# Batch 0 of a hash-masked attention: the fifth chunk's weight sums to TensorE, key-bit copies and mask products from VectorE to ScalarE

## The chip, the cores and the metric

The kernel runs on one core of a Trainium2 chip. The metric is device microseconds (us) of one execution. Engines are named as in the profile: PE (TensorE), PEld (its weight loads), DVE (VectorE), ACT (ScalarE), POOL (GpSimd) and SP (SyncE, which here only issues DMAs). Each engine works through its own instructions in program order, and engines meet through semaphores.

## The reference

Four batches, eight heads, 768 positions, head width 64. Six random projections give each query and key a six-bit bucket; a query sees only the keys of its own bucket.

```python
q_bits = (np.einsum('bhsd,dk->bhsk', q, proj) > 0)      # k_bits alike
mask = q_bucket[:, :, :, None] == k_bucket[:, :, None, :]
scores = scale * np.matmul(q, k.transpose(0, 1, 3, 2))
scores = np.where(mask, scores, -1000000000.0)
attn = softmax(scores); out = attn @ v
...
u = x + real(fft2(x))                 # x: (4, 768, 512), the heads side by side
un = (u - mean(u)) / sqrt(var(u) + 1e-6)
return u + relu(un @ w_ch1) @ w_ch2   # 512 -> 2048 -> 512
```

The first half is the attention, the second a Fourier mixing with a two-layer network behind it.

## The kernel before

**The whole.** The four batches follow each other. Attention works on pairs of heads: pair number n = 4 b + t, for t = 0 to 3. While the attention of batch b runs, the Fourier mixing and the network of batch b-1 are threaded between its steps. Batch 0 has no such partner, so its attention is threaded with the arrival of w_ch1 (`weights1`, line 728). Batch 0 is the stage that the change touches. It stands inside `manual_schedule` (line 1534): for PE, DVE, ACT and POOL the order is the one in which the Python code issues the instructions, and a scheduler has no say. From batch 1 on a scheduler orders them.

**One step of attention.** A pair has six steps, c = 0 to 5, one for each chunk of 128 keys. In a step:

- PE computes the scores of the chunk against all 768 queries, in two halves g of 384 queries. For each half and each of the two heads there is first a bf16 matmul of the bit rows (line 938), which adds a large constant where buckets agree, and then the fp32 score matmul (line 946). Both go to one PSUM tile `sc`, of which there are two, so half g of a step cannot start until ACT has read the same half of the step before.
- ACT takes the exponential of each half (line 950) into `pk`, of which there are two buffers. Where buckets differ the result is zero.
- DVE adds the new weights into `acc` (line 1041), in two halves. From c = 1 to 4 it does so in batch 0; the last chunk, c = 5, is not added but summed by PE.
- PE multiplies the weights with the values (line 967), one step late: in step c it does the products of chunk c-1, after the scores of chunk c.

So PE's order is: scores c, products c-1, then whatever else the step brings, then scores c+1. After the sixth chunk (in the first step of the next pair) ACT copies the products out (lines 977 and 980), PE sums `acc` and the last `pk` over the keys with a matrix of ones (line 985), and DVE turns the sums (line 992) and takes their reciprocals; a step later ACT copies these into place (line 1001), and DVE scales the output (lines 1002 and 1006).

**Preparing the next pair** (`prepare`, line 807) is threaded into steps 1 to 4 of the pair before, one part a step: DVE transposes q (c = 1) and k (c = 2) (line 820); then for q (c = 3) and for k (c = 4) PE computes the projections (line 854) and DVE turns them into bits (line 858). Pairs 0 to 4 are prepared in a light way (`LITE`): the bits of q are multiplied with the two columns of `own`, which leave a large number or zero (line 864, two instructions), and the bits of k are copied with 32-row blocks exchanged (line 870, four instructions). The scores of the next pair need the q products and the k bits for half g = 0, and the copies for half g = 1.

**Arrival of w_ch1.** The weights come as raw 64-bit words. Each of 16 slices is turned into fp32 by two bit operations on DVE (lines 639 and 643), a conversion of the low word on ACT (line 647), and an addition on DVE (line 649) that needs ACT's part. A slice is converted in four of five steps. After four slices PE sums columns of w_ch1 (`ws`, line 673), ACT copies the sums (`part`, line 678), PE averages (`wm`, line 681), and DVE subtracts the mean (line 687). In batch 0 this happens in pair 0 and pair 1 as they end; for the other two column blocks PE's part follows when the attention of batch 0 is over.

**Small PSUM tiles.** The bit projections, `ws`, `wm` and the sums take turns in two PSUM buffers (`pt`, line 520), so each waits until the tile two places earlier has been read.

**Pair 3** has one thing more on DVE: the first half of the Fourier folding, 3.2 us ahead of the q bits of pair 4 and 3.2 us ahead of its k bits (`fold`, lines 1099 to 1117).

The order of one step is set here:

```python
pk = weigh(n, c)                 # scores, exponentials
...                              # additions into acc
for sc in scales: next(sc, None)
while pending: finish()          # products of the chunk before
pending.append((n, c, pk, oos, sums))
if c > (3 if b == 1 else 2): next(half, None)     # fold, pair 3
if c > 0: next(ahead, None)                       # prepare(n + 1)
yield                                             # -> one slice of w_ch1
```

Of the kernel before, what the change touches and what calls it, by code (L numbers as in the profile page):

```python
# [16 lines left out]
AF = mybir.ActivationFunctionType  # L17
ALU = mybir.AluOpType
AX = mybir.AxisListType

P = 128
B, H, S, D = 4, 8, 768, 64
# [3 lines left out]
NT = S // P  # L26
NPAIR = H // 2
HALF = S // 2
# [457 lines left out]
def _main(  # L486
# [33 lines left out]
    def pt(shape, name):  # L520

        turn[0] += 1
        if roomy[0] and turn[0] % 2:
            if turn[0] % 4 == 1:
                return ps_o.tile(shape, F32, tag="o", name=name)
            return ps_sc.tile(shape, F32, tag="sc", name=name)
        return ps_1.tile(shape, F32, tag="ps", name=name)
# [279 lines left out]
    def prepare(n):  # L807

        lite = n in LITE
        ts = {}  # L810
        for io, nm in enumerate("qk"):
            tn = nat.pop((nm, n))
            tt = wt([P, S], F32, nm + "t", f"{nm}t{n}")
            if n > 0:
                to, at = tt, tn
                if nm == "q":

                    to = tt.rearrange("p (i r n) -> p r i n", i=2, r=2)
                    at = tn.rearrange("p (r i n) -> p r i n", i=2, r=2)
                nc.vector.transpose(to, at)  # L820
            for g in range(2) if n == 0 else ():
                ps = pt([P, 3, P], f"tr{nm}{n}_{g}")
                for i in range(3):
                    c = 2 * i + g if nm == "q" else 3 * g + i
                    nc.tensor.transpose(ps[:, i, :], tn[:, c * P : (c + 1) * P], ident)
                if nm == "q":
                    for i in range(2):
                        dst = tt[:, i * HALF + g * HALF // 2 : i * HALF + (g + 1) * HALF // 2]
                        evac(
                            dst.rearrange("p (j c) -> p c j", c=3),  # L830
                            ps[:, :, i * D : (i + 1) * D],
                        )
                else:
                    evac(
                        tt[:, g * HALF : (g + 1) * HALF],
                        ps.rearrange("p c t -> p (c t)"),
                    )
            ts[nm] = tt
            yield
            if n >= LATER:  # L840
                norm(n, io, tn)
        if lite:

            qk = wt([P, 2, S], BF16, "qb", f"qkb{n}")
            qz = qk[:, 0].rearrange("p (g s) -> p g s", g=2)
            bits = {"q": qz[:, 0], "k": qk[:, 1, 0:HALF]}
            for io, nm in enumerate("qk"):  # L850
                ps = pt([P, HALF], f"bits{nm}{n}")
                for j in range(4):
                    h, g = divmod(j, 2)
                    nc.tensor.matmul(
                        ps[32 * j : 32 * j + 32, :], pjw[:, h * D : h * D + 32],
                        ts[nm][:, g * HALF : (g + 1) * HALF], start=True, stop=True,
                    )
                nc.vector.tensor_scalar(
                    bits[nm], ps, 0.0, off[:, io : io + 1],
                    op0=ALU.is_gt, op1=ALU.subtract,  # L860
                )
                if io == 0:
                    for g in (1, 0):
                        nc.vector.tensor_scalar(
                            qz[:, g], qz[:, 0], own[:, g : g + 1], None, op0=ALU.mult
                        )
                else:
                    for j in range(4):
                        to, at = (slice(32 * i, 32 * i + 32) for i in (j, j ^ 1))
                        nc.vector.tensor_copy(qk[to, 1, HALF:S], qk[at, 1, 0:HALF])  # L870
                yield
            preps[n] = ts["q"], ts["k"], qk, None
            return

        ps = pt([P, HALF], f"bits{n}")
        for j in range(4):
            src = ts["qk"[j // 2]][:, (j % 2) * HALF : (j % 2 + 1) * HALF]
            nc.tensor.matmul(
                ps[32 * j : 32 * j + 32, :], pj, src, start=True, stop=True
            )  # L880
        bt = wt([P, HALF], BF16, "bt", f"bt{n}")
        nc.vector.tensor_scalar(bt, ps, 0.0, None, op0=ALU.is_gt)  # L882
        yield

        qb = wt([P, 2, S], BF16, "qb", f"qb{n}")
        kb = wt([P, 2, NT], F32, "kb", f"kb{n}")
        for h in range(2):
            ps = ps_sc.tile([P, 2, 512], F32, tag="sc", name=f"qb{n}_{h}")
            for g in range(2):
                rows = slice(32 * g, 32 * g + 32)  # L890
                with behind() if g + h else nullcontext():
                    last[0] = nc.tensor.matmul(
                        ps[:, g, 0:HALF], pw[rows, h, :], bt[rows, :],
                        start=True, stop=True,
                    )
            evac(qb[:, h, :].rearrange("p (g s) -> p g s", g=2), ps[:, :, 0:HALF])
        ps = ps_sc.tile([P, 2, 512], F32, tag="sc", name=f"kb{n}")
        for c in range(NT):
            g, i = divmod(c, NT // 2)
            rows = slice(64 + 32 * g, 96 + 32 * g)  # L900
            with behind() if c else nullcontext():
                last[0] = nc.tensor.matmul(
                    ps[:, g, 2 * i : 2 * i + 2], bt[rows, i * P : (i + 1) * P],
                    pw[rows, :, 0], start=True, stop=True,
                )
        nc.vector.tensor_copy(
            kb.rearrange("p h (g i) -> p g i h", g=2),
            ps[:, :, 0:NT].rearrange("p g (i h) -> p g i h", h=2),
        )
        preps[n] = ts["q"], ts["k"], qb, kb  # L910
# [58 lines left out]
                    pk[:, g, h, 0:w], start=(c == 0), stop=(c == NT - 1),  # L969
                )  # L970

    def scale(n, oos, sums):


        x = xs[n // NPAIR][:, n % NPAIR]
        vs = wt([P, 1], F32, "vs", f"vs{n}")
        nc.scalar.copy(vs, oos[0][:, HALF : HALF + 1])
        halves = [x[:, g * HALF : (g + 1) * HALF] for g in range(2)]
        for g, xg in enumerate(halves):
            nc.scalar.activation(xg, oos[g][:, 0:HALF], AF.Identity, bias=vs)  # L980

        ps = pt([P, HALF], f"sum{n}")
        for i, part in enumerate(sums):
            for j in range(4):
                nc.tensor.matmul(
                    ps[32 * j : 32 * j + 32, :], ones, part[:, j // 2, j % 2],
                    start=(i == 0), stop=(i == len(sums) - 1),
                )


        rt = wt([P, S], F32, "rt", f"rt{n}", 1)
        nc.vector.transpose(rt[:, 0:HALF], ps)  # L992
        rc = wt([P, HALF // 32], F32, "rc", f"rc{n}")
        nc.vector.tensor_scalar(rc, rt[:, 0:HALF:32], S * EPS, None, op0=ALU.add)
        nc.vector.reciprocal(rc, rc)
        yield
        rr = wt([P, 2, HALF // 32], F32, "rr", f"rr{n}")
        for g in range(2):
            for i in range(4):
                j = 2 * g + i // 2  # L1000
                nc.scalar.copy(rr[32 * i : 32 * i + 32, g], rc[32 * j : 32 * j + 32])
        nc.vector.transpose(
            rt.rearrange("p (j i) -> p j i", i=32),
            rr.rearrange("p g j -> p (g j)")[:, :, None].broadcast_to([P, S // 32, 32]),
        )
        nc.vector.tensor_tensor(x, x, rt, op=ALU.mult)

    def attention(b):
        xs[b] = wt([P, NPAIR, S], F32, "x", f"x{b}")
        pending, scales = [], []  # L1010

        def finish():
            n, c, pk, oos, sums = pending.pop(0)
            with behind() if n >= NPAIR and t is not None else nullcontext():
                values(n, c, pk, oos)
            if c == NT - 1:
                scales.append(scale(n, oos, sums))
                next(scales[-1])

        for t in range(NPAIR):  # L1020
# [8 lines left out]
            for c in range(NT):  # L1029
# [2 lines left out]
                sums = [acc]  # L1032
                if c == 0:
                    first = new
                elif c == NT - 1 and b == 0:

                    sums.append(new)
                else:

                    for g in (0, 1) if b == 0 else (slice(0, 2),):  # L1040
                        nc.vector.tensor_tensor(  # L1041
                            acc[:, g], (first if c == 1 else acc)[:, g], new[:, g],
                            op=ALU.add,
                        )
# [590 lines left out]
```

## Time and profile before

| what | value |
|---|---|
| three runs | 1115.38, 1116.21, 1119.01 us; median 1116.21 |
| the profiled execution: its time | 1115.38 us |
| the profiled execution: span from the first to the last instruction | 1113.5 us |
| granted clock of PE over the span | 0.989 |
| instructions in the span | 14,170 |
| first scores of pair 0 | 11.71 us after the start |
| first scores of pair 4 (batch 1) | 119.27 us after the start |

The median of the runs lies 0.8 us above the profiled execution. Its time is 1.9 us more than its span; that part is outside the instructions.

A line of the timeline gives the start, the time that it covers, the engine, the line of the kernel, the operation, what is written and read, the shapes, how many instructions are merged, and in brackets how long the engine sat idle before it and whom it waited for. A line of the waits gives the waiting engine and line, the one waited for, then the total in us, the number of waits and the longest. In a table of stretches, each engine has its busy time and, in brackets, its instructions; behind them stands the granted clock. Matmuls overlap, so PE's busy time does not say how much of its time is used; the distance from the start of a group to the start of the next one does. A group of four score matmuls of one half of a step takes 0.81 us this way, with the bit matmuls inside it.

### The profile page before, as it was taken

How to read it: one execution, taken by the hardware profiler on the slowest of the kernel's cores; microseconds unless marked ns; L12 is line 12 of the kernel's file. 1: busy time of each engine (PE TensorE's matmuls, PEld its weight loads, DVE VectorE, ACT ScalarE, POOL GpSimd, SP SyncE). 2: the span in 40 equal slices, each digit the busy share in tenths (PEclk: the TensorE clock that was granted, in tenths of full speed). 3: DMA queues.
4: the chain of work that ended last, by engine and by line, in shares of the span. 5: the costliest groups of instructions: out<-in, count | busy, mean ns of one | idle time of the engine just before them, and what ended most of it. 6: DMA issues, size and time to landing. Idle time of an engine off the chain costs nothing. (4 is left out here: it accounts for less than half of the span.)

```text
span 1113.5 us, 14170 instructions
## 1 busy us (share of the span) xinstructions
PE 1050.3 (94%) x4933; PEld 632.6 (57%) x4933; DVE 789.8 (71%) x1336; ACT 499.8 (45%) x1055; POOL 76.2 (7%) x164
## 2 busy tenths in 40 slices
PE   7899897899999999999999999999899999899996
PEld 3333354447644675555754685545564579568675
DVE  6889969768798968767767867776476785444353
ACT  4555455562376233545145324454635423851420
POOL 0000000001000120010000020010200012400000
PEclk9989999999999999999999999999999999999999
DMA  9754362540156260323153160323542206732401
GB/s 237 221 90 103 57 173 68 193 105 1 38 138 217 57 194 11 67 76 67 56 142 88 39 186 31 62 62 95 174 162 64 65 24 229 260 112 78 131 20 41
DMA packets 179295, 117.82 MB, mean 106 GB/s; under 512 B 130064, under 2 KB 163472, under 8 KB 179216
## 3 DMA queue, kind: packets, MB, share of 16 engines
q1 hardware_dynamic: 169840, 88.65, 29.7%
q0 software_dynamic: 7808, 27.79, 7.7%
q8 instruction: 41, 0.67, 0.3%
q10 hardware_dynamic: 1568, 0.39, 0.2%
q14 instruction: 38, 0.31, 0.1%
HBM read 95.82 MB, written 20.97 MB: 105 GB/s over the span
## 5 line engine op out<-in xcount | busy, mean ns | idle before, releaser
L1323 PE MATMUL o<-w,h 128*128 128x256 f32 x1152 | 262.1, 384 | 5.3 <-DVE rt L992 1.9
L1323 PEld LDWEIGHTS o<-w,h 128*128 128x128 f32 x1152 | 217.1, 191 | 50.4 <-issue 4.0
L950 ACT ACTIVATE pk<-sc 128x768 f32<-128x768 f32 x192 | 149.6, 810 | 100.1 <-PE sc L946 79.2
L1443 PE MATMUL h_p<-x,w 128*128 128x384 f32 x448 | 165.3, 498 | 4.8 <-ACT h L1465 3.7
L946 PE MATMUL sc<-qt,kt 64*128 64x384 f32 x768 | 155.9, 508 | 4.5 <-ACT pk L950 4.2
L967 PE MATMUL oo<-pk,vn 128*64 128x385 f32 (+1 forms) x768 | 155.6, 502 | 4.3 <-DVE pk L956 3.6
L956 DVE SCALAR_TENSOR_TENSOR pk<-qb,kb,pk 128x768 f32<-128x768 bf16 x132 | 129.0, 1012 | 39.2 <-ACT pk L950 35.6
L1443 PEld LDWEIGHTS h_p<-x,w 128*128 128x128 f32 x448 | 82.4, 192 | 73.2 <-ACT h L1465 7.5
L1443 PE MATMUL h_p<-w 128*128 128x384 f32 x288 | 106.3, 491 | 6.5 <-ACT w L1480 3.4
L1041 DVE TENSOR_TENSOR acc<-acc,pk 128x1536 f32<-128x1536 f32 (+1 forms) x72 | 105.7, 1482 | 5.7 <-ACT pk L950 5.2
L967 PEld LDWEIGHTS oo<-pk,vn 128*64 128x64 f32 x768 | 49.7, 137 | 99.1 <-issue 73.7
L946 PEld LDWEIGHTS sc<-qt,kt 64*128 64x128 f32 x768 | 67.0, 188 | 50.8 <-issue 24.5
L1443 PEld LDWEIGHTS h_p<-w 128*128 128x128 f32 x288 | 53.8, 191 | 46.7 <-ACT w L1480 5.4
L1335 DVE SCALAR_TENSOR_TENSOR w<-o,rs,w 128x256 f32<-128x256 f32 x56 | 26.7, 478 | 39.0 <-PE o L1323 38.9
L1353 ACT COPY tq<-o 128x256 f32<-128x256 f32 x24 | 8.9, 371 | 94.2 <-PE o L1323 94.2
L1469 DVE TENSOR_TENSOR h<-h 128x384 f32<-128x384 f32 x32 | 17.8, 557 | 40.9 <-ACT h L1468 40.9
L1323 PE MATMUL o<-w 128*128 128x256 f32 x176 | 42.3, 383 | 1.3 <-DVE w L1335 1.3
L1476 DVE TENSOR_TENSOR h<-h 128x384 f32<-128x384 f32 x32 | 17.7, 553 | 32.5 <-ACT h L1475 32.4
L1077 POOL DMA_DIRECT2D out_dram<-w x30 | 16.4, 548 | 334.9 <-DVE w L1335 184.4
L1323 PEld LDWEIGHTS o<-w 128*128 128x128 f32 x176 | 32.8, 190 | 8.8 <-DVE w L1335 2.9
L1342 ACT COPY tq<-o 128x256 f32<-128x256 f32 x24 | 8.9, 370 | 60.6 <-PE o L1323 60.5
L1139 PE MATMUL cs<-ch,z 128*128 128x128 f32 (+3 forms) x192 | 32.3, 318 | 2.3 <-DVE bt L882 1.9
(175 smaller groups left out, 1330.6 us busy)
## 6 DMA issues: line engine op xcount, KB each, us to landing
w<-ad SPq DMA_DIRECT2D x168, 128.0 KB, 2.0
w<-bd SPq DMA_DIRECT2D x42, 512.0 KB, 4.5
zraw<-in_moe_w_ch_dram POOLq DMA_DIRECT2D x16, 512.0 KB, 4.1
zlast<-in_moe_w_ch_dram POOLq DMA_DIRECT2D x16, 512.0 KB, 5.1
bd<-w SPq DMA_DIRECT2D x14, 512.0 KB, 3.6
vn<-in_v_dram SPq DMA_DIRECT2D x32, 192.0 KB, 3.5
qn<-in_q_dram SPq DMA_DIRECT2D x120, 48.0 KB, 2.4
kn<-in_k_dram SPq DMA_DIRECT2D x60, 96.0 KB, 3.3
```

What stands on the lines that cost most here:

```text
L946: last[0] = nc.tensor.matmul(ps[:, h, 0:HALF], kt[rows, ks], qt[rows, qs], start=kb is not None, stop=True,)
L950: nc.scalar.activation(pk[:, g, :, 0:HALF], ps[:, :, 0:HALF], AF.Exp, scale=SCALE)
L956: nc.vector.scalar_tensor_tensor(w, qb[:, h].rearrange("p (g s) -> p g s", g=2), kb[:, h, c : c + 1], w, op0=ALU.is_equal, op1=ALU.mult,)
L967: nc.tensor.matmul(oos[g][h * D : (h + 1) * D, 0:w], nat["v", n][:, (2 * c + h) * D : (2 * c + h + 1) * D], pk[:, g, h, 0:w], start=(c == ...
L1041: nc.vector.tensor_tensor(acc[:, g], (first if c == 1 else acc)[:, g], new[:, g], op=ALU.add,)
L1077: (nc.sync if b == B - 1 else nc.gpsimd).dma_start(out[b, s0 : s0 + 2 * w - 1 : 2, cols], src[at : at + w, cols])
L1139: nc.tensor.matmul(ps[:, pc + 2 * lo : pc + 2 * hi - 1 : 2], z[:, cp, pc, par, t * P : (t + 1) * P], ch[:, cp, pc, lo:hi], start=(cp == 0) ...
L1323: nc.tensor.matmul(ps, a[:, r], right7[i][:, r], start=start and r == 0, stop=r == HF // 2 - 1, skip_group_check=not start,)
L1335: nc.vector.scalar_tensor_tensor(t[:, cols], src, r, t[:, cols], op0=ALU.mult, op1=ALU.add)
L1443: nc.tensor.matmul(ps, left[:, k], right[i][:, k], start=start and k == 0, stop=k == 1, skip_group_check=not start,)
L1469: nc.vector.tensor_tensor(c21, c12, c21, op=ALU.add)
L1476: nc.vector.tensor_tensor(c22, c21, c22, op=ALU.add)
```

## The change

In batch 0 three kinds of work change engine. The two products of the q bits with the columns of `own` and the four copies of the k bits become ACT instructions, in all five lightly prepared pairs. The additions of the fifth chunk (c = 4) into `acc` are left out for the four pairs of batch 0; PE sums that chunk with the matrix of ones instead, into the PSUM tile that later takes the sums of `acc` and of the sixth chunk. That tile is taken one step earlier than before.

```diff
                 if io == 0:
                     for g in (1, 0):
-                        nc.vector.tensor_scalar(
-                            qz[:, g], qz[:, 0], own[:, g : g + 1], None, op0=ALU.mult
+                        nc.scalar.activation(
+                            qz[:, g], qz[:, 0], AF.Copy, scale=own[:, g : g + 1]
                         )
                 else:
                     for j in range(4):
                         to, at = (slice(32 * i, 32 * i + 32) for i in (j, j ^ 1))
-                        nc.vector.tensor_copy(qk[to, 1, HALF:S], qk[at, 1, 0:HALF])
+                        nc.scalar.copy(qk[to, 1, HALF:S], qk[at, 1, 0:HALF])
...
+    def weight_sums(ps, sums, first, last):
+
+        for i, part in enumerate(sums):
+            for j in range(4):
+                nc.tensor.matmul(
+                    ps[32 * j : 32 * j + 32, :], ones, part[:, j // 2, j % 2],
+                    start=first and i == 0, stop=last and i == len(sums) - 1,
+                )
+
-    def scale(n, oos, sums):
+    def scale(n, oos, sums, ps=None):
...
-        ps = pt([P, HALF], f"sum{n}")
-        for i, part in enumerate(sums):
-            for j in range(4):
-                nc.tensor.matmul(
-                    ps[32 * j : 32 * j + 32, :], ones, part[:, j // 2, j % 2],
-                    start=(i == 0), stop=(i == len(sums) - 1),
-                )
+        fresh = ps is None
+        if fresh:
+            ps = pt([P, HALF], f"sum{n}")
+        weight_sums(ps, sums, fresh, True)
...
+            if b == 0 and c == NT - 2:
+                total.append(pt([P, HALF], f"sum{n}"))
+                weight_sums(total[0], sums[:1], True, False)
             if c == NT - 1:
-                scales.append(scale(n, oos, sums))
+                scales.append(scale(n, oos, sums, total.pop() if total else None))
...
                 if c == 0:
                     first = new
+                elif c == NT - 2 and b == 0:
+                    sums = [new]
                 elif c == NT - 1 and b == 0:
```

The short description of the change also names late tests and squares (the range tests of the raw words, line 663, and the squares, line 802). In the order of the two programs' instructions these stand at the same places. What differs there: DVE has 10 products, 20 copies and 8 additions fewer; ACT has the 10 products and 20 copies more; PE has 16 sum matmuls more; on SP the transfers of finished parts of w_ch1 to DRAM stand a little earlier among the loads of pairs 3 to 5. In ACT's order, the products for the next pair stand behind the exponentials of c = 3 and ahead of those of c = 4 (in pairs 0 and 2 with one conversion of line 647 between them), and the copies stand behind the exponentials of c = 4 and ahead of those of c = 5.

## The prediction, on record before the result was known

> **What bounds the kernel now.** I read the page first: which engine is busy, and where in the span it is not.
>
> ```profile
> PE 1050.3 (94%) x4933; PEld 632.6 (57%) x4933; DVE 789.8 (71%) x1336; ACT 499.8 (45%) x1055; POOL 76.2 (7%) x164
> PE   7899897899999999999999999999899999899996
> DVE  6889969768798968767767867776476785444353
> ```
>
> PE has its gaps in the first eight slices, 220 us; behind them it is full nearly everywhere. The change lies in the first 125 us. What it does to the time is what it does to PE there, since a full PE passes a delay on to the end. Next, the table of stretches for batch 0:
>
> ```profile
> 30.00:60.00 30.00, 26.72 (x170) 9.80 (x170) 26.94 (x47) 15.88 (x31) 0.00 (x0) 0.91 0.69 182
> 60.00:90.00 30.00, 28.27 (x178) 10.44 (x174) 26.53 (x45) 17.65 (x32) 0.00 (x0) 0.96 0.47 78
> 90.00:113.50 23.50, 23.50 (x162) 9.01 (x164) 21.18 (x36) 13.46 (x26) 0.11 (x1) 0.96 0.52 120
> 113.50:124.30 10.80, 6.58 (x44) 2.03 (x38) 9.71 (x21) 4.85 (x14) 0.00 (x0) 1.00 0.65 116
> ```
>
> PE (first), and DVE (third) are both near 90%, ACT (fourth) near 55%. That speaks for moving work from DVE to ACT. The seventh number, the granted clock, is below 1: 30 x 0.09 + 30 x 0.04 + 23.5 x 0.04 = 4.8 us lost to half rate. Whom PE waits for, from 11.5 to 125 us:
>
> ```profile
> PE ws L673 <- DVE qkb L858: 4.9, 2, 3.3
> PE sc L938 <- DVE qkb L858: 2.8, 2, 1.7
> PE ws L673 <- DVE rt L992: 1.5, 1, 1.5
> PE wm L681 <- ACT part L678: 1.1, 1, 1.1
> ```
>
> So DVE does stop PE: 3.28 us at 52.5, 1.73 us at 85.7, and 1.61 + 1.51 + 1.10 = 4.2 us behind the last pair. The half rate came after the first two: a group of line 946 that takes 0.81 us took 1.49 at 57.95 and 1.70 at 88.49. But what counts is where DVE's late instruction stands in the queue. The timeline of pair 2's end:
>
> ```profile
> 79.52 1.62 ACT L950 ACTIVATE pk<-sc 128x768 f32<-128x768 f32 x2 [1.70 <-PE sc L946]
> 80.15 1.78 DVE L1041 TENSOR_TENSOR acc<-acc,pk 128x768 f32<-128x768 f32 x2
> 81.03 0.68 ACT L647 ACTIVATE fraw<-fraw 128x512 int32<-128x512 uint32 x1
> 81.85 0.61 DVE L858 TENSOR_SCALAR qkb<-bitsq,off 128x384 bf16<-128x384 f32 x1
> 82.43 0.34 PE L938 MATMUL sc<-qkb 64*128 64x384 bf16 x2
> 82.50 0.68 DVE L864 TENSOR_SCALAR qkb<-qkb,own 128x384 bf16<-128x384 bf16 x2
> 86.72 0.61 DVE L858 TENSOR_SCALAR qkb<-bitsk,off 128x384 bf16<-128x384 f32 x1
> 87.39 0.34 PE L938 MATMUL sc<-qkb 64*128 64x384 bf16 x2 [1.73 <-DVE qkb L858]
> ```
>
> ACT does the exponentials of c = 4 at 79.52, while DVE still adds c = 3; the q bits (line 858) end only at 82.46. PE's scores of c = 5 start at 82.43 on a PSUM tile that those exponentials have long freed.
>
> **The wait that is added.** In the new ACT order the products stand between the exponentials of c = 3 and c = 4. ACT must wait for the q bits, so the exponentials of c = 4, which PE needs for the tile of the c = 5 scores and then for the products of c = 4, come after them. The q bits won't come sooner: the products, copies and c = 4 additions all stand behind them in DVE's order. From the turning of the last pair's sums (line 992, which waits for PE: 37.20, 68.34 and 94.05) to the q bits DVE runs without a gap and loses nothing by the change, and PE's way starts from the same sums. So the lag between the two is read straight from before. In pair 0 it hangs on a DMA (line 647 waits 3.1 us, to 22.8), also unchanged.
>
> Price of a product on ACT: no row has it. Below: DVE's own row.
>
> ```profile
> L864 DVE TENSOR_SCALAR qkb<-qkb,own x10: 319/319/321, 10.5 to 109.9; 128x384 bf16<-128x384 bf16 x10
> ```
>
> Above: ACT's instruction of that shape with one operand by partition.
>
> ```profile
> L980 ACT ACTIVATE x<-oo,vs x8: 573/581/586, 35.3 to 112.7; 128x384 f32<-128x384 f32 x8
> ```
>
> I take 0.58, the same engine and shape; two in series (the second reads what the first reads and overwrites it) are 1.16. [...] A copy of 32 x 384 is between 0.20 (line 1001, 32 x 12) and 0.48 (line 537, 128 x 384 on ACT); I take 0.45, since length decides between these rows and it has the longer's: 1.8 for four.
>
> From the q bits to the first half of the c = 4 exponentials: products 1.16, a conversion 0.68 in pairs 0 and 2, one half 0.81.
>
> - Pair 0: bits end 27.26, + 2.65 = 29.9; scores of c = 5 at 28.22: wait 1.7. Of this 0.5 is already late from the start: the last copy of pair 0 ends 4 x 0.45 behind the products, near 13.2, not at 12.75.
> - Pair 1: 55.73 + 1.97 = 57.7; PE stands until 55.79 for `ws`, on the same q bits, as before, then needs 1.0: wait 0.9.
> - Pair 2: 82.46 + 2.65 = 85.1 against 82.43: wait 2.7.
> - Pair 3: the fold's 3.2 us lie ahead of the bits: 109.47 + 1.97 = 111.4 against 108.14: wait 3.3.
>
> Sum 8.6 us. Then three smaller things. `wm` of pair 0 gets the buffer of the sums, so it waits for line 992: 37.83 in place of 37.07, 0.8. In pair 3 the k bits end at 115.64 - 1.74 - 0.6 = 113.3, copies 115.1, c = 5 exponentials 115.9 and 116.7; PE is through scores, products and sums at 115.2: 0.8 for its next products. In pairs 0 to 2 the copies fit before the scores of c = 5 end or shortly after, and a conversion covers it: nothing, at most 0.7 a pair.
>
> **The sums on PE.** 16 matmuls, four start to start 0.67 (35.64 to 36.31 on line 985): 4 x 0.67 = 2.7, on PE's path.
>
> **What goes.** DVE loses 10 x 0.32 + 20 x 0.25 + 8 x 0.95 = 15.8 us. PE gets back only what stood behind them: 1.73 at 85.7 (k bits of pair 3; they now end about 85.7, and PE comes later), 0.4 of small waits for copies, and 3.7 of the 4.2 behind pair 3, where PE now comes last (0.5 stays: sums to `part` 4.2 on ACT, PE has 3.6 to do). Sum 5.8. The 3.28 stays. Loads on SP that change place end long before use: nothing.
>
> **Half rate.** Of the 4.8 us, the first stretch (pair 1) stays, that of 88.6 goes (1.7), and the new stops of 2.7 and 3.3 bring one each, as 1.73 did: + 1.7. Stops of 1.61 and 1.51 brought none, so pair 0 gets none. [...]
>
> **Sum.** 8.6 + 0.8 + 0.8 + 2.7 - 5.8 + 1.7 = +8.8. On the profiled execution 1115.4 + 8.8 = 1124.2; the median of the runs lies 0.8 higher: 1125.0. With products at 0.32 and copies at 0.20 the four waits are 0.5 less each, 2.1, as is the start, 0.4, and the last 0.8 goes: 1121.7. With two more half-rate stretches (1.7 each) and 0.7 for copies in two pairs: 1130.
>
> **Rivals.**
>
> - The relief wins (faster). If the products never held the exponentials up, only 2.7 + 0.8 against 5.8 and perhaps the 3.4 of pair 1 would count: -2.3 to -5.7, 1110.5 to 1114. It decides if the q bits end 2.65 (pairs 0, 2) or 1.97 us (1, 3) ahead of PE's c = 5 scores. For it: DVE is at 90% and loses 15.8. Against it: the margins now are 1.0, 1.1, 0.0 and -1.3. 0.14.
> - It cancels out (within 0.3%, about what a measurement of this kernel tells from no change). Lower bound of the prices, no new half rate, and part taken up by PE's later gaps (3.57 at 220, 1.93 at 138): 1117 to 1119. Against it: those gaps wait for DVE and ACT, not for a transfer with a clock of its own. 0.14.
> - Slower than forecast: each stop breeds half rate, and with it the next lag: 1131 to 1135. 0.06.
> - My case: 0.66.
>
> Range: 1115 to 1131. It leaves out most of the faster rival and the upper part of the last one, under 2 in 10 together, and takes in both ends of the unknown prices (1121.7 and 1130). Faster 0.14, same 0.14, slower 0.72.
>
> **What would show it.** Right: ACT idle ahead of line 864 for DVE's line 858, four times, most in pair 3; PE waiting at line 938 for ACT's line 950; `wm` waiting for line 992 in pair 0; first scores of pair 4 about 8 us later than 119.27; DVE below 80% in 30 to 113. Wrong: products near 0.3; q bits well earlier against PE than now; later gaps of PE shorter by the same 8 us.

## The result and the profile after

The changed kernel takes 1127.9 us in the median of five runs (1125.37 to 1129.37), the kernel before 1115.96 beside it (1113.99 to 1119.01): a ratio of 1.0104 with a 95% interval of 1.0082 to 1.0127. It is slower, as forecast, by 12 us where 9 had been forecast. One run of the kernel before beside the later experiments, 1514.5 us at a granted clock of 0.655 where its other runs have 0.979 or more, is left out throughout. The profiled execution of the changed kernel took 1127.9 us with a span of 1125.7, 12.2 more than the span before. In the profile of after, lines from 972 on are shifted by up to 10; the additions into `acc` are now L1051, the turning of the sums L997, the sums L976.

From the page of after, the busy times and two rows of slices:

```profile
PE 1055.1 (94%) x4965; PEld 634.6 (56%) x4965; DVE 774.5 (69%) x1298; ACT 514.4 (46%) x1085; POOL 76.3 (7%) x164
PE   7989798989989999999999999999899999899996
DVE  5677767969598977676768777785566785444353
```

DVE has lost 789.8 - 774.5 = 15.3 us of work (15.8 were counted), ACT has gained 14.6; the 32 rows more on PE are the 16 sum matmuls, two rows each. The relief took place, and PE's first slices are no fuller. The same in the stretches of batch 0:

```profile
30.00:60.00 30.00, 25.40 (x174) 9.58 (x177) 21.46 (x34) 17.80 (x35) 0.00 (x0) 0.97 0.68 187
60.00:90.00 30.00, 27.38 (x174) 10.30 (x168) 21.71 (x35) 20.42 (x39) 0.00 (x0) 0.92 0.44 80
90.00:113.50 23.50, 22.46 (x158) 8.73 (x155) 18.18 (x32) 14.39 (x29) 0.11 (x1) 1.00 0.50 124
```

DVE (third) fell from near 90% to 72, 72 and 77%, yet PE (first) does less in each stretch than before. An engine with more room, and the bound engine slower: the trouble must be a wait. PE's waits of after from 11.5 to 140 us:

```profile
PE sc L938 <- ACT pk L950: 7.9, 4, 3.3
PE ws L673 <- DVE qkb L858: 3.3, 1, 3.3
```

The first line is new. In the profile of before, PE never waited for an exponential at a bit matmul in this stretch (a second profile of that kernel has one such wait, of 0.27 us). And ACT's own waits in the same stretch begin with

```profile
ACT qkb L864 <- DVE qkb L858: 24.4, 4, 8.6
```

so ACT, which works 46% of the time, stands 24.4 us in batch 0 ahead of the products, with the exponentials of c = 4 queued behind them. The end of pair 2 in the timeline, the place that the prediction showed for before:

```profile
84.65 1.78 DVE L1051 TENSOR_TENSOR acc<-acc,pk 128x768 f32<-128x768 f32 x2
...
86.35 0.61 DVE L858 TENSOR_SCALAR qkb<-bitsq,off 128x384 bf16<-128x384 f32 x1
...
87.00 1.26 ACT L864 ACTIVATE qkb<-qkb,own 128x384 bf16<-128x384 bf16 x2 [5.25 <-DVE qkb L858]
...
88.16 0.64 ACT L647 ACTIVATE fraw<-fraw 128x512 int32<-128x512 uint32 x1
88.71 1.50 ACT L950 ACTIVATE pk<-sc 128x768 f32<-128x768 f32 x2
...
89.56 0.34 PE L938 MATMUL sc<-qkb 64*128 64x384 bf16 x2 [2.56 <-ACT pk L950]
```

One reads it from the bottom: PE waits 2.56 us for the first half of the c = 4 exponentials, these stand behind a conversion and two products, the products wait for the q bits, and the q bits stand on DVE behind the additions of c = 3, which the change leaves where they were.

### Where the 12 us arose

I set the start of each PE instruction of after against the same instruction of before; I call the difference the lag. It is +0.3 us at the first transposes, ahead of any work that the change moves, +1.3 after the first scores, +3.7 at the end of pair 0 (36 us of before), +4.5 in pair 2 (72), +7.1 at its c = 5 scores, +4.4 in pair 3 (104), +7.8 at that pair's c = 5 scores, +10.4 by the end of that pair's products, and +6.9 at the first scores of pair 4, which are at 126.19 us. So batch 0, the only stage in which the program differs, costs 6.9 us. From there to 240 us the lag grows to 11.4, and then stays between 11 and 12 to the end (12.1 at 1090). This second part, nearly 5 us, lies in a stretch whose instructions are almost the same ones in the same order.

### The profile page after: what moved, and what is told of

Its sections match the earlier page's. It is cut to its first block, busy times and chain, and to the rows that moved or that the text cites. A ratio compares the mean times of both kernels' runs of the same rounds, so it can differ in the third digit from the quotient of the medians.

```text
span 1125.7 us, 14210 instructions
## 1 busy us (share of the span) xinstructions
PE 1055.1 (94%) x4965; PEld 634.6 (56%) x4965; DVE 774.5 (69%) x1298; ACT 514.4 (46%) x1085; POOL 76.3 (7%) x164
## 5 line engine op out<-in xcount | busy, mean ns | idle before, releaser
L967 PE MATMUL oo<-pk,vn 128*64 128x385 f32 (+1 forms) x768 | 156.8, 503 | 2.2 <-DVE pk L956 1.8
L967 PEld LDWEIGHTS oo<-pk,vn 128*64 128x64 f32 x768 | 49.7, 137 | 98.1 <-issue 73.7
L1051 DVE TENSOR_TENSOR acc<-acc,pk 128x1536 f32<-128x1536 f32 (+1 forms) x64 | 98.4, 1549 | 7.3 <-ACT pk L950 6.8
```

The lines of the kernel that those rows point to most:

```text
L967: nc.tensor.matmul(oos[g][h * D : (h + 1) * D, 0:w], nat["v", n][:, (2 * c + h) * D : (2 * c + h + 1) * D], pk[:, g, h, 0:w], start=(c == ...
L1051: nc.vector.tensor_tensor(acc[:, g], (first if c == 1 else acc)[:, g], new[:, g], op=ALU.add,)
```

## The experiments

Three theories stand in the expectations below. **A**: it is ScalarE's order; the exponentials of c = 4 are blocked behind products whose bits are late. **B**: it is the work, which is dearer on ScalarE. **C**: it is the ones matmuls on TensorE and the PSUM tile that they hold. Kernels that ran side by side share their runs of before (median 1117.0 for e1 to e4, 1117.07 for e5 to e8, 1117.09 for e9 and e10). Each profile is one execution; those of e3 and e5 were not typical, 4.3 us above and 4.8 us below the median of their kernels. "Lag" at 131 us below is that of the first matmul of the Fourier step (L1139 before, at 130.7); it is +6.7 for the changed kernel.

### The three parts one by one

e1 is the changed kernel with products and copies back on VectorE, so that only the sums on TensorE remain:

```diff
-                        nc.scalar.activation(
-                            qz[:, g], qz[:, 0], AF.Copy, scale=own[:, g : g + 1]
+                        nc.vector.tensor_scalar(
+                            qz[:, g], qz[:, 0], own[:, g : g + 1], None, op0=ALU.mult
...
-                        nc.scalar.copy(qk[to, 1, HALF:S], qk[at, 1, 0:HALF])
+                        nc.vector.tensor_copy(qk[to, 1, HALF:S], qk[at, 1, 0:HALF])
```

> Only the fifth chunk's sums move to PE; products and copies stay on DVE. Theory A (the loss comes from ACT's order: exponentials queued behind products and copies that wait for DVE's late bits): nothing of that is left, so the relief shows: the 1.73 us stop of pair 3 and its half rate (1.7) go, some 3 of the 4.2 us behind pair 3 go, 16 matmuls add 2.7; first scores of pair 4 near 115.5 us, time 1110 to 1114 us. Theory C (the sums on PE's path, or the PSUM tile held a step longer, cost the time): 1118 to 1122 us.

Measured: 1114.28 us, ratio 0.9963 (0.9942 to 0.9984), lag -1.6 at 131. C falls: the sums alone are a small gain. The gain is smaller than theory A had it, with the first scores of pair 4 at 117.6 us and not near 115.5: in pair 0 PE stops for 1.49 us at the scores of c = 4, behind an exponential that stands behind a conversion (L647), which waits 4.59 us for a slice of w_ch1 (3.12 before, without such a stop). e2, e5, e6 and e10 have the same stop, 1.30 to 1.85 us; why the slice comes later there is not settled.

e2 is the kernel before with only the products on ScalarE (the first half of the diff above, reversed), e3 with only the copies there (the second half, reversed).

> Only the ten products move to ACT. Theory A: the q bits come as late as before, so ACT stands for them four times and PE stops at the scores of c = 5 for about 2, 0, 2.6 and 3.3 us; the copies and additions still on DVE keep the stop at pair 3; time 1120 to 1125 us. Theory B (the loss is the work itself: 16.4 us more on ACT, of which the products are 6.2): 1119 to 1121 us, with the exponentials late by the products' own 1.2 us only.

> Only the twenty copies move to ACT, which then stand ahead of the exponentials of c = 5. Theory A: they wait for the k bits, and these are later than in the whole change, since the additions of c = 4 and the products are still ahead of them on DVE (in pair 3 the second part of the fold as well): PE waits some 2.5, 0, 6 and 8 us at the ends of the pairs, more than in the whole change; time 1126 to 1135 us. Theory B: by work, 10.2 of the 16.4 us on ACT: 1121 to 1124 us.

Measured: e2 1122.72 us, 1.0042 (1.0022 to 1.0062), lag +4.8 at 131; e3 1133.74 us, 1.0134 (1.0109 to 1.016), lag +17.1. In e2 the stops at the c = 5 scores are those of the whole change, 2.55 in pair 2 and 3.31 in pair 3. e2's time lies within what A gave, but its interval (some 1119.5 to 1124 us) reaches into what B gave, so its time alone doesn't part the two; e3 does, since 20 copies of 0.51 us can't take 17 us of TensorE's time by their length. In e3 the copies stand between the exponentials of c = 4 and c = 5, and the k bits are later still, because the products and the c = 4 additions are on VectorE ahead of them. Pair 3 in its timeline, ACT:

```profile
115.87 1.62 ACT L950 ACTIVATE pk<-sc 128x768 f32<-128x768 f32 x2 [2.27 <-PE sc L946]
126.32 2.07 ACT L870 COPY qkb<-qkb 32x384 bf16<-32x384 bf16 x4 [8.83 <-DVE qkb L858]
128.41 1.51 ACT L950 ACTIVATE pk<-sc 128x768 f32<-128x768 f32 x2
```

ACT stands for 8.83 us, then the copies, then the exponentials for which PE's products (L967) have waited 7.26 us. The three parts alone give -2.7, +5.7 and +16.7 us, which doesn't add up to the whole's 12: with the copies moved alone, the products and the c = 4 additions stay on VectorE ahead of the k bits.

### The same work in another order

e4 is the changed kernel with one `yield` moved up, so that products and copies are issued one step after their bits: on ScalarE the products stand behind the exponentials of c = 4, the copies behind those of c = 5. No work leaves its engine.

```diff
                     op0=ALU.is_gt, op1=ALU.subtract,
                 )
+                yield
                 if io == 0:
...
                         nc.scalar.copy(qk[to, 1, HALF:S], qk[at, 1, 0:HALF])
-                yield
```

> The whole change with one yield moved: each engine has the same instructions, but on ACT the products stand behind the exponentials of c = 4 and the copies behind those of c = 5. Theory A: the stops of 1.8, 2.6 and 3.3 us at the scores of c = 5 go; the later start (1.3) stays, and the copies hold the second half of the next pair's first scores for 0 to 1.5 us; time 1114 to 1120 us. Theory B: the same work on ACT, so 1124 to 1130 us.

Measured: 1115.2 us, ratio 0.9975 (0.9955 to 0.9996), lag -2.9 at 131. The whole loss of 12 us is gone with the same instructions on the same engines: theory A, and B falls. The end of pair 2 in the timeline of e4, ACT:

```profile
81.16 1.62 ACT L950 ACTIVATE pk<-sc 128x768 f32<-128x768 f32 x2 [1.70 <-PE sc L946]
84.14 1.26 ACT L865 ACTIVATE qkb<-qkb,own 128x384 bf16<-128x384 bf16 x2 [1.36 <-DVE qkb L858]
85.31 0.67 ACT L647 ACTIVATE fraw<-fraw 128x512 int32<-128x512 uint32 x1
85.88 1.49 ACT L950 ACTIVATE pk<-sc 128x768 f32<-128x768 f32 x2
```

The products still wait for the bits, 1.36 us, but PE doesn't wait for ACT at the c = 5 scores, here or in any other pair of batch 0: the c = 4 exponentials have been done.

e10 puts the products alone in the later place, on the kernel before:

```diff
                 if io == 0:
+                    yield
                     for g in (1, 0):
-                        nc.vector.tensor_scalar(
-                            qz[:, g], qz[:, 0], own[:, g : g + 1], None, op0=ALU.mult
+                        nc.scalar.activation(
+                            qz[:, g], qz[:, 0], AF.Copy, scale=own[:, g : g + 1]
...
                         nc.vector.tensor_copy(qk[to, 1, HALF:S], qk[at, 1, 0:HALF])
-                yield
+                    yield
```

> The kernel before, with the products alone on ScalarE and in the later place (behind the c=4 exponentials); the sums and the copies stay on VectorE as they were. Nothing is left out. Against e2, which has the same work with the products in the change's place, it tells the price of the place alone; against e5 the worth of the ones matmuls. Theory A: no ScalarE stop at the c=5 scores, 0 to 4 us faster than before (1113 to 1117), 6 to 9 us under e2's 1122.7. Rival (0.61 us of ScalarE in place of 0.32 of VectorE costs wherever it stands): 1119 to 1123.

Measured: 1114.87 us, 0.9978 (0.996 to 0.9997), lag -2.0 at 131. Against e2 it is the same ten instructions in another place, and 7.9 us less. ACT's wait for the q bits, first in e2, then in e10:

```profile
ACT qkb L864 <- DVE qkb L858: 22.3, 4, 8.3
```

```profile
ACT qkb L865 <- DVE qkb L858: 8.4, 4, 4.1
```

### Faster than both

e5 has the sums on TensorE, the products on ScalarE in the later place, and the copies on VectorE (in `prepare`, e10's lines on top of the sums). e6 leaves pair 0's products on VectorE as well, so that nothing at the start changes:

```diff
-                    yield
+                    if n > 0:
+                        yield
                     for g in (1, 0):
+                        if n > 0:
+                            nc.scalar.activation(
...
+                        else:
+                            nc.vector.tensor_scalar(
+                                qz[:, g], qz[:, 0], own[:, g : g + 1], None, op0=ALU.mult
+                            )
+                    if n == 0:
+                        yield
```

> The changed kernel with the ones matmuls of chunk 4 left on TensorE and the products left on ScalarE, but issued one step later, behind the c=4 exponentials, as in e4; the copies are back on VectorE, where they keep their old place. Nothing is left out. Theory A (ScalarE's order is what costs): no PE stop at c=5 scores in pairs 0 to 3, batch 0 ends 4 to 5 us earlier than before's 131, the whole time 1110 to 1114. Rival (the work costs wherever it stands, or the copies must leave VectorE as well): not under e4's 1115, as VectorE keeps 16 copies of 0.20 us each ahead of the next pair's first scores, so 1115 to 1119.

> As e5, but pair 0's products also stay on VectorE, so that the first scores don't wait for two 0.61 us products on ScalarE. Theory A with the start as a cost of its own: first scores at 11.3 us as before instead of 12.0, and 0.7 to 1.3 us less than e5. Rival (the start's delay is absorbed by the first slices of w1, for which the exponentials wait anyway in pair 0): within 0.5 us of e5.

Measured: e5 1113.93 us, 0.9973 (0.995 to 0.9996); e6 1113.12 us, 0.9966 (0.9949 to 0.9983). Both are faster than the kernel before, and by some 14 us faster than the change. They are within what theory A gave, at its upper end; but e1, e4 and e10 lie within some 2 us of them, so these runs don't tell which of the five is best. The copies that e5 leaves on VectorE take 0.25 us each there (L870 before), not the 0.20 of the expectation. That pair 0's products cost anything at the start is not shown: 0.8 us between e5 and e6 is less than either interval, and the first scores start at 11.94 us in e5 and at 12.12 in e6, where 11.3 had been expected for e6 "as before"; the two profiles of before have 11.71 and 11.95.

### The five microseconds behind batch 0

e7 and e8 are the changed kernel and the kernel before, unchanged, each for a second profile. e9 is the changed kernel with the later place in one preparation alone, that of pair 4 beside pair 3 (`if n == NPAIR: yield` ahead of the work, in place of the `yield` behind it).

> The changed kernel once more, for a second profile. If the 5 us that it lost behind batch 0 (between 131 and 225 us) belong to the change, its first scores of pair 4 are again near 126.2 us, PE stops again for over 3 us near 178 us behind ScalarE's wait for a slice of the second weights, a half rate of 7 to 10 us follows, and the lag on before grows from 7 at 131 us to 11 or 12 at 240. If they were chance of one execution, the stop or the half rate is absent and the lag at 240 is 7 to 9.

> The kernel before once more, for a second profile. If its smooth passage from 131 to 225 us belongs to it, there are again no PE stop over 2 us and no half rate between 130 and 220 us, and its PE instructions lie within 1 us of the first profile's times at 240. If that passage was chance, a stop of about 3 us near 170 with a half rate behind it appears, and its time at 240 is 3 to 5 us later.

> The changed kernel, with the later place for products and copies (as in e4) in the last of batch 0's preparations alone, that of pair 4 beside pair 3; the other three stay as the change has them. Nothing is left out. Theory A, each stop paid for where it stands: the PE stop of 3.32 us at pair 3's c=5 scores goes, those of pairs 0 and 2 stay near 1.8 and 2.6, batch 0 ends 3 to 5 us before the changed kernel's, at lag +2 to +4 on before. If the further 4 to 5 us that the changed kernel lost from 131 to 225 us come from the late start of batch 1, they go too: 1118 to 1122 in all. If they come from the slices of the second weights or from anything else that doesn't care for pair 3's order, they stay: 1122 to 1126.

Measured: e7 (1127.45 us) repeats its kernel: lag +7.5 at 131, a stop of 2.88 us at 179, half rate (a granted clock of 0.5) from 181.6 us for 10.2 us, +11.4 at 240. e8 (1117.49 us) doesn't repeat in every point: it is 2.4 us ahead of the first profile at 131, because it has 3.4 us of half rate in batch 0 where the first had 10.2 (6.8 from 54.5 and 3.4 from 88.6), and it has one at 172 us that the first lacked; so what before does there is partly chance. Measured against it, the first profile of the changed kernel is 9.1 us late at 131 and 12.7 at 240: how the 12 us divide between batch 0 and what follows depends on the execution by 2 us. e9 takes 1120.96 us, 1.0048 (1.0023 to 1.0073): 6.9 less than the whole change. Pair 3's stop of 3.32 is gone, those of pairs 0 and 2 remain (1.37 and 2.56), the lag is +2.2 at 131 and +3.8 at 240. So one order in one pair was worth 4.5 us where it stands and, in these profiles, 3 more behind it.

What grows behind batch 0 is time at half rate. Between 130 and 245 us, the growth of the lag from 131 to 240 us beside the time at half rate, of which the first profile of before has 3.4 us:

| kernel | lag at 131 | lag at 240 | growth | half rate, 130 to 245 |
|---|---|---|---|---|
| changed kernel, e7 | +6.7, +7.5 | +11.4, +11.4 | +4.7, +3.9 | 13.7, 13.7 |
| e3 | +17.1 | +21.8 | +4.7 | 14.0 |
| e4, e10 | -2.9, -2.0 | -0.3, +0.1 | +2.6, +2.1 | 10.2, 10.2 |
| e1 | -1.6 | -0.3 | +1.3 | 13.7 |
| e2, e8, e6 | +4.8, -2.4, -2.9 | +6.1, -1.3, -4.0 | +1.3, +1.1, -1.1 | 6.8, 6.8, 6.8 |
| e9 | +2.2 | +3.8 | +1.6 | 3.4 |
| e5 | -5.2 | -7.3 | -2.1 | 0 |

At a granted clock of 0.50 a stretch of 3.4 us loses 1.7 us of full rate, by an estimate from these two numbers. The changed kernel has 10.2 us more of it than before, 5.1 by this estimate, and grew by 4.7. Between the same two places, with the same 437 matmul rows, PE was busy for 100.2 us against 96.5 before, and idle for 13.8 against 12.8: about 1 us of the growth is more waiting, the rest is slower matmuls. It is no chance of one profile either: one minus the granted clock, times the span, is on average 17.6 us over the five runs of the changed kernel and 11 us over the 70 of before (and over the eight of e9). Broadly half rate and growth go together, but not case by case. In e1, e2, e4, e5 and e6 PE also stops for 1.8 to 2.2 us at the scores of pair 4 (at 138 us in e2, from 128 to 132 in the others), behind exponentials for which ACT waits 5.8 to 6.1 us until VectorE has added the weights before (L1051 in e1); before, ACT waited 4.5 us there and PE did not stop. Ahead of the half rate, in the changed kernel, stand a stop of 2.53 us at 146 (PE for VectorE's bits, L882; 1.93 before) and one of 3.37 at 178, where an exponential stands on ScalarE behind a conversion (L647) that waits 3.61 us for a slice of the second weights; before, there were two stops of 1.09 and 1.93 with work between them. Why that slice came so late (issued at 171.45, used at 180.28, against 163.02 and 169.55) is not settled; e9, which comes to it 7 us earlier, stops for 2.43 there and gets no half rate.

## Why the prediction was right, and where its sizes were off

The direction, the mechanism and the place were right, and the time was within the range; the excess was forecast at 8.8 us and is 12.2 between the two profiled spans.

- **Waits at the c = 5 scores**, forecast 1.7, 0.9, 2.7 and 3.3. Measured 1.83, none, 2.56 and 3.32 us; in e7 1.45, 0.93, 2.57 and 3.32. In the first profile pair 1's wait was hidden by a half rate that slowed PE in front of it (a granted clock of 0.50 from 58.11 to 64.94 us; the scores start at 61.45). This term, the largest, held in three of four pairs, and e4 shows that it hangs on the order.
- **Prices on ACT**, taken as 0.58 and 0.45. The rows of after:

```profile
L864 ACT ACTIVATE qkb<-qkb,own 128x384 bf16<-128x384 bf16 x10 | 6.1, 615 | 26.2 <-DVE qkb L858 26.1
L870 ACT COPY qkb<-qkb 32x384 bf16<-32x384 bf16 x20 | 10.2, 509 | 1.3 <-DVE qkb L858 1.1
```

  0.615 and 0.509 us: both a little over the row that I took as the upper one (0.581 of L980 and 0.479 of L537). The higher price of the products moves the sum by 0.1 us a pair.
- **The start**, forecast as 0.5 within pair 0's wait. Measured 1.3, of which 0.3 is there at the first transposes and not of the change; PE stops 0.72 at the second half, as the copies end at 14.08 and not near 13.2. The change's part, 1.0, is twice what was forecast.
- **`wm` of pair 0 gets the buffer of the sums**, 0.8. It fails: `wm` starts at 40.73, right behind the sums and ahead of L997 (40.87), so it did not wait for that tile. Why not was not followed up.
- **Copies ahead of pair 3's products**, 0.8. No such wait is in the trace: PE came later than counted.
- **The sums on PE**, 2.7. The lag steps by 0.6 to 0.8 at each of the four groups: held.
- **What goes**, 5.8. The stop of 1.73 in pair 3 is gone (the lag falls by 1.4 net of the sums), and those of 1.61 and 1.51 behind pair 3; the 1.1 at `wm` stays. Some 4.6 to 5.
- **Half rate**, +1.7. This is the step that was mis-sized. In batch 0 it came out near 0 (that of 88.6 is gone, 1.9; a new one at 116.1 costs 1.8; the stop of 2.56 in pair 2 brought none). That 88.6 would go was luck in part: the second profile of before has none there. Over the whole run the changed kernel has 35.8 us at half rate against 26.9, and the 10.2 more between 130 and 245 us were not in the sum at all. The prediction had held that a full PE passes a delay on to the end; in fact it passed on 6.9, and the later stops brought about 5 more.

With the terms as measured, batch 0 is 1.3 + 1.8 + 2.6 + 3.3 of waits (9.0), + 2.7 of sums, - 4.8 of stops that went, about 0 of half rate: 6.9. So the 8.6 of waits came out almost right because the start, too small, and pair 1, too large, made up for each other, and without the time lost behind batch 0, which was not forecast, the total would have been some 2 us below the sum. That rest is mostly the half rate that the table above shows.

The rivals: that the relief wins fell with the order, and is true for another order of the same work (e4, -0.25%). That it cancels was wrong: PE's idle time behind batch 0, to 240 us, didn't shrink (12.8 and 13.8 us). The gap of 3.57 fell to 2.75, but two stops ahead of it grew, from 0.29 and 0.49 to 0.98 and 1.27, and so did the two early ones of batch 1, from 0.37 and 1.93 to 1.35 and 2.53. That each stop breeds half rate, at 0.06, was the nearest to what came on top, though the stretches lie behind batch 0 and not in it.

## What to carry to other kernels

Before an instruction is moved to an idler engine, ask what stands behind it in that engine's order and when its input comes: here ten 0.6 us products cost 6 us in one place and less than nothing one step later. The busy share of the two engines, 90 against 55%, said nothing about it; the distance from the late input to the next instruction that the bound engine needs gave the three stops that came to within 0.2 us, though not the half rate behind them. If such work must move, issue it behind the instruction that the bound engine waits for next, and try the parts alone, since the loss of one can hide the gain of another.

## What the runs showed of the hardware

**In these traces half rate went by windows of 3.41 us that did not move with the program.** The granted clock was 0.50 in them, and a group of four score matmuls that takes 0.81 us at 1.00 took 1.51 (at 61.72 us of after). In every trace the stretches are multiples of 3.41 us (but for the last, which the end of the trace cuts off) and start on one grid, whose offset against the program differs from execution to execution: the last edge ahead of 60 us lies at 58.11 us in after and at 57.89 in before. In the profile of after they start at 58.11, 116.14, 150.27, 180.99 and 966.06 us: the others lie 17, 27, 36 and 266 times 3.4133 us behind the first. Over the 12 profiled executions (from the first record of the clock, 10 to 12 us after the start, to 1095 us, ahead of the last writes) I added up PE's idle time in each window of the grid that ran at full rate. The ends of matmuls are modelled, so a count can be off by one or two: after a window with 1.0 to 1.65 us idle none of 148 went to half rate next, with 1.65 to 2.0 it was 21 of 40, with over 2.0 all 43. So the same stop can bring it or not. Two executions of before with the same stop of 1.73 us, the window with the stop and the next one (the seventh number is the granted clock):

```profile
85.20:88.61 3.41, 1.69 (x13) 0.59 (x11) 3.29 (x8) 0.65 (x2) 0.00 (x0) 1.00 0.00 0
88.61:92.03 3.42, 3.42 (x11) 1.19 (x12) 3.08 (x6) 1.72 (x4) 0.00 (x0) 0.50 0.00 0
```

```profile
83.15:86.56 3.41, 1.73 (x10) 0.48 (x8) 3.26 (x5) 1.73 (x3) 0.00 (x0) 1.00 0.02 2
86.56:89.97 3.41, 3.36 (x20) 1.31 (x20) 3.12 (x8) 2.03 (x4) 0.00 (x0) 1.00 0.00 0
```

And a longer stop of 2.53 us that the changed kernel and e9 share (PE at the Fourier step for L882). In the changed kernel one window takes most of it, and the next is at half rate; in e9 it falls on two windows, and nothing follows:

```profile
146.86:150.27 3.41, 1.75 (x13) 1.46 (x14) 1.60 (x2) 0.86 (x3) 0.00 (x0) 1.00 0.87 269
150.27:153.69 3.42, 3.42 (x15) 2.38 (x16) 0.00 (x0) 1.17 (x4) 0.00 (x0) 0.50 0.55 154
```

```profile
139.50:142.91 3.41, 2.07 (x12) 1.44 (x8) 3.38 (x6) 1.14 (x3) 0.00 (x0) 1.00 0.01 3
142.91:146.32 3.41, 2.22 (x17) 1.93 (x18) 1.14 (x2) 0.65 (x2) 0.00 (x0) 1.00 1.00 298
146.32:149.74 3.42, 3.42 (x23) 1.45 (x23) 0.52 (x1) 2.27 (x4) 0.00 (x0) 1.00 0.43 122
```

From these counts (64 of the 83 windows with over 1.65 us idle) my estimate is that a prediction for this kernel can say that stops of 2 to 3 us will bring some half rate, but not which of them will: the stop of 2.56 us at 87.0 us in the changed kernel lies across the edge at 88.83 us and brought none, that of 2.55 in e2 (85.3 to 87.9) fell almost whole into one window, and half rate followed at 87.61. Half rate also goes with most of the scatter of this kernel: over the 70 runs of before that stand beside the experiments the time goes from 1108.8 to 1123.1 us, the granted clock from 0.979 to 0.997, and the two go against each other (correlation -0.82).
